# Attention with a learned position bias and a gated FFN on one Trainium2 core: where the split halves are made, how the PSUM places are cut, and bias rows computed by distance

## The chip, the cores and the metric

One core of a Trainium2 chip. The metric is the device time of one execution in microseconds (us); the kernel before has a median of 694.9 us over three runs.

## The reference, cut to what matters

Four batches, eight heads, 576 positions, 64 per head, all in fp32. The bias of a score depends on the query position i, on the distance |i - j| and on the head alone, so it is the same for all batches. The FFN has 2304 tokens, 512 in and out, 2048 hidden.

```python
scores = scale * np.matmul(q, k.transpose(0, 1, 3, 2))
psi_rel = np.log1p(np.abs(pos[:, None] - pos[None, :]))
psi_i = np.log1p(np.maximum(pos[:, None], 1.0))
x = (psi_rel / psi_i)[..., None]
h = np.maximum(x @ w1 + b1, 0.0)          # w1: 1 x 32
bias = h @ w2                             # w2: 32 x 8
scores = scores + bias.transpose(2, 0, 1)[None]
attn = softmax(scores)                    # sum + 1e-9
x = np.matmul(attn, v)                    # to 2304 x 512
h = x @ w_in
g = h * np.clip(h + 3.0, 0.0, 6.0) / 6.0
out = g @ w_out
```

## The kernel before, in words

**Engines.** PE is TensorE, DVE is VectorE, ACT is ScalarE, POOL is GpSimd, SP issues most loads. Where a product needs fp32 accuracy, both factors are split into a high and a low half (fp16, or the type `F32R` for q and k) and PE does three products: high x high, high x low, low x high. `high_part` (lines 117 to 123) makes a high half on POOL ("P"), DVE ("D") or ACT (any other letter); `low_part` (L140) makes a low half on DVE in one instruction, full x scale - high.

**Tiles.** The work is a list of softmax tiles n of 128 rows x 576 columns. First come rows 0 to 255 of the four batches, in units of one head pair with four tiles, then rows 256 to 575 of the four batches, in units with five tiles, the last of which holds 64 rows of each head. The rows 0 to 255 of batches 0 and 1 are "direct" tiles: `soft_max` (L559, DVE) adds the bias to the scores and takes the row maximum, `soft_exp` (L570, ACT) the exponential, PE turns the tile in fp32 through PSUM (`t_ps`), ACT copies it back. All 112 other tiles are normalised and split: `soft_norm` (L578, L582 on DVE, then the high half `hl`), `soft_low` (low half, L140), and `soft_turn` (L635) turns both by a DMA. Which engine makes `hl` follows the letters of `CFG['hl']`, tile by tile: 'AP' is ACT and POOL in turns.

**q and k** of a unit that is not direct come as one tile `st` of 832 (rows 0 to 255) or 896 columns. One tile ahead of the unit each, `split_qk_a` makes the high half `qkh` on ACT (L406), `split_qk_b` the low half `qkl` on POOL in two pieces, 576 columns of k and 256 or 320 of q (L413), and `split_qk_c` the two 64-column pieces `tq` of the last tile, on ACT (L426) and POOL (L427).

**The FFN** `ffn` (L736) of one batch and 256 or 320 tokens is a generator that is stepped from the main loop. The first layer has 16 hidden tiles of 12 matmuls `h_ps` (L781); for each, `post` issues ACT `t` (L771), DVE `t` (L764), ACT `g` (L758) and POOL `g` (L760). The second layer has 4 x 48 matmuls `o_ps` (L804). The first FFN is special: its second layer must wait until w_out is prepared, at whose end DVE forms `r_w2c`, the row ratios of w_out, with which the 16 tiles `g` are scaled again.

**Bias rows.** 36 groups of 16 query rows are computed once. `T` holds the table w1 x log1p|j - 572| over 1148 columns. `z_group` (L846 on DVE, L850 on ACT) makes four z tiles of 576 columns from shifted views of T, each with four query rows x 32 hidden units on its partitions; `bias_mm` (L863) multiplies them with w2, in fp32 (two passes, so 16 records a group), `bias_out` (L879) brings the result out of PSUM on ACT, `bias_store` writes it to tables `bias_d` in DRAM and `load_bias` loads 128 rows of a head pair on SP when a tile needs it. `bias_step` and `bias_next` do one step of this chain; the main loop calls them by the rates `rb` and others of `CFG`.

**PSUM** has 8 banks. `open_psum` begins with three double places (tag "s": scores, `t_ps`, bias) and two single places (tag "w": `h_ps`, `o_ps`, `pv_ps`). `open_banks` closes these and opens two double and four single places; from then on bias groups take two single places.

**Order.** The main loop runs `front(n)` and `back(n)` for each tile n, with FFN and bias steps between by credits. `START` = 21 opens the first FFN. At `SWITCH` = 37 `open_steady` runs what is left of the first FFN, opens the four single places and keeps PE's order as written from there; up to then a scheduler sorts each engine's instructions by priority.

```python
        if n == START:
            open_ffn()
        if n == cfg["psw"]:
            open_banks()
        if n == SWITCH:
            open_steady()
```

Of the kernel before, what the change touches and what calls it, by code (L numbers as in the profile page):

```python
# [1254 lines left out]
```

## Time and profile before

| | |
|---|---|
| runs | 693.82, 694.9, 696.72 us; median 694.9 |
| profiled execution, span | 690.7 us |
| PE busy | 640.2 us, 93% |
| DVE, ACT busy | 486.6 and 487.5 us, 70 and 71% |
| POOL busy | 261.1 us, 38% |
| largest groups on PE | `h_ps` 200.9 us, `o_ps` 195.5 us |
| bias groups on PE | `b_ps` 45.1 us of records, four column groups side by side |

The span is one execution as the hardware profiler took it on this core, from its first instruction to its last; the runs are timed without it. "PEld" is the loading of weights, which runs beside matmuls. An idle time is put down to what ended it. PEclk is the clock that TensorE was granted, as a share of its full one.

### The profile page before, as it was taken

The page shows a single profiled execution, that of the slowest core. Times are in us where ns is not written, and L with a number is a line of the kernel's source. Part 1 is how long each engine was busy: PE and PEld are TensorE (multiplying, and loading weights), DVE is VectorE, ACT ScalarE, POOL GpSimd, SP SyncE. Part 2 cuts the span into 40 slices and gives each one's busy share as a digit, 9 for nine tenths or more (in the row PEclk, how much of TensorE's full clock was granted, in tenths as well). Part 3 has the DMA queues.
Part 4 walks back from the last instruction along what each step waited for, and adds up shares of the span by engine and source line. Part 5 has one row for each costly group of instructions (what it writes and reads, how often), then busy time and mean ns, then how long its engine had stood idle before and what let it go on. Part 6 is the DMA issues. An engine that isn't in the chain of part 4 may idle for free. (4 is left out here: it accounts for less than half of the span.)

```text
span 690.7 us, 15099 instructions
## 1 busy us (share of the span) xinstructions
PE 640.2 (93%) x5552; PEld 453.1 (66%) x5552; DVE 486.6 (70%) x1150; ACT 487.5 (71%) x970; POOL 261.1 (38%) x322
## 2 busy tenths in 40 slices
PE   7688899787899999899989999999999999999998
PEld 2234456564587667578878877777767777777775
DVE  7889977999737977577778777876688668731310
ACT  7986768987739977697568857886688657832620
POOL 1111125756114532255335634653265425420420
PEclk9998999998999999999999999999999999999999
DMA  8899769651856798979999989787968795730000
GB/s 295 297 329 345 263 246 366 234 194 32 259 162 147 188 251 178 256 180 196 237 266 232 232 186 206 149 184 154 242 123 184 159 198 120 114 66 25 1 10 28
DMA packets 175737, 130.13 MB, mean 188 GB/s; under 512 B 137520, under 2 KB 144944, under 8 KB 174640
## 3 DMA queue, kind: packets, MB, share of 16 engines
q1 hardware_dynamic: 165872, 113.84, 66.0%
q10 hardware_dynamic: 9792, 15.34, 7.4%
q8 instruction: 43, 0.70, 0.4%
q14 instruction: 30, 0.25, 0.1%
HBM read 77.24 MB, written 15.34 MB: 134 GB/s over the span
## 5 line engine op out<-in xcount | busy, mean ns | idle before, releaser
L781 PE MATMUL h_ps<-x,wi 128*128 128x256 f16 (+1 forms) x1536 | 200.9, 288 | 8.7 <-DVE t L764 6.0
L804 PE MATMUL o_ps<-g,wo 128*128 128x256 f16 (+1 forms) x1536 | 195.5, 286 | 2.0 <-ACT g L123 1.3
L781 PEld LDWEIGHTS <-wi 128*128 128x128 f16 x1536 | 147.4, 98 | 60.9 <-issue 20.1
L804 PEld LDWEIGHTS <-wo 128*128 128x128 f16 x1536 | 147.3, 98 | 47.4 <-issue 10.5
L760 POOL TENSOR_TENSOR g<-t,g 128x256 f16<-128x256 f32 (+1 forms) x128 | 105.6, 834 | 154.9 <-ACT g L758 153.4
L570 ACT ACTIVATE bt<-bt,sm 128x576 f32<-128x576 f32 x144 | 110.6, 768 | 57.0 <-DVE sm L559 53.7
L140 DVE SCALAR_TENSOR_TENSOR hl<-bt,sm,hl 128x576 f16<-128x576 f32 x112 | 99.2, 900 | 30.1 <-ACT hl L123 14.7
L764 DVE SCALAR_TENSOR_TENSOR t<-t,t,h_ps 128x320 f32<-128x320 f32 (+1 forms) x112 | 56.0, 515 | 40.3 <-ACT t L771 39.2
L117 POOL TENSOR_SCALAR hl<-bt,sm 128x576 f16<-128x576 f32 x56 | 47.4, 847 | 94.9 <-DVE sm L582 30.1
L758 ACT ACTIVATE g<-t 128x256 f16<-128x256 f32 (+1 forms) x128 | 55.4, 438 | 31.8 <-DVE t L764 30.9
L559 DVE CUSTOM_DVE_ANT_0 bt<-s_ps,bt 128x576 f32<-128x576 f32 x88 | 64.5, 751 | 10.8 <-PE s_ps L527 5.4
L771 ACT ACTIVATE t<-h_ps,t,hr 128x320 f32<-128x320 f32 (+1 forms) x112 | 64.1, 586 | 6.1 <-PE h_ps L781 4.2
L413 POOL TENSOR_TENSOR qkl<-st,qkh 128x576 fp32r<-128x576 f32 (+2 forms) x48 | 57.9, 1229 | 24.3 <-ACT qkh L406 18.6
L863 PE MATMUL b_ps<-z_e,w_sb 128*32 128x288 f32 x448 | 45.1, 430 | 12.3 <-ACT bo L879 5.1
L814 ACT ACTIVATE ot<-o_ps,os 128x256 f32<-128x256 f32 (+1 forms) x32 | 15.9, 496 | 56.6 <-PE o_ps L804 51.4
L123 ACT ACTIVATE hl<-bt,sm 128x576 f16<-128x576 f32 x56 | 43.0, 770 | 7.2 <-DVE sm L582 4.2
L578 DVE TENSOR_SCALAR sm<-sm 128x1 f32<-128x1 f32 x112 | 16.7, 150 | 44.4 <-ACT bt L570 44.0
L846 DVE TENSOR_SCALAR z_e<-T,nbp 128x576 f32<-128x576 f32 x69 | 39.6, 622 | 11.6 <-PE b_ps L863 11.5
L879 ACT ACTIVATE bo<-b_ps,cv_sb,isc 128x288 f32<-128x288 f32 (+1 forms) x54 | 35.7, 663 | 2.9 <-DMA bias<-bo 2.0
L863 PEld LDWEIGHTS b_ps<-z_e,w_sb 128*32 128x32 f32 x448 | 14.8, 111 | 32.3 <-ACT z_e L850 6.6
L253 POOL TENSOR_SCALAR w<-w 128x1024 f32<-128x1024 f32 x8 | 10.8, 1348 | 65.3 <-ACT wo L252 52.9
L850 ACT ACTIVATE z_e<-T,bp 128x576 f32<-128x576 f32 x43 | 32.4, 771 | 3.9 <-DVE bp L1037 2.9
(125 smaller groups left out, 902.1 us busy)
## 6 DMA issues: line engine op xcount, KB each, us to landing
bt<-bias SPq DMA_DIRECT2D x36, 576.0 KB, 5.3
bias<-bo ACTq DMA_DIRECT2D x36, 288.0 KB, 5.6
w<-in_w_in_dram SPq DMA_DIRECT2D x8, 1024.0 KB, 7.2
vs<-in_vp_dram SPq DMA_DIRECT2D x24, 320.0 KB, 5.0
st<-in_qk_dram SPq DMA_DIRECT2D x16, 448.0 KB, 4.5
wo<-in_w_out_dram SPq DMA_DIRECT2D x5, 1024.0 KB, 5.1
bt<-bias SPq DMA_DIRECT2D x16, 288.0 KB, 3.6
qk<-in_qkd_dram SPq DMA_DIRECT2D x8, 544.0 KB, 8.9
```

The lines of the kernel that those rows point to most:

```text
L117: nc.gpsimd.tensor_scalar(out=out, in0=full, scalar1=scale, scalar2=1.0, op0=ALU.mult, op1=ALU.mult)
L140: nc.vector.scalar_tensor_tensor(out=out, in0=full, scalar=scale, in1=high, op0=ALU.mult, op1=ALU.subtract)
L413: nc.gpsimd.tensor_sub(out=lo[:, c:c + w], in0=t[:, c:c + w], in1=hi[:, c:c + w].bitcast(F32))
L559: nc.vector.tensor_tensor_reduce(out=halves(bt), in0=ps, in1=halves(src), op0=ALU.add, op1=ALU.min, scale=-0.125, scalar=3.0e38, accum_out ...
L570: nc.scalar.activation(out=bt, in_=bt, func=AF.Exp, scale=-1.0, bias=sm[:, 0:1], accum_out=total)
L758: nc.scalar.activation(out=g[:, 0], in_=uu, func=AF.Copy)
L760: e.tensor_sub(out=g[:, 1], in0=uu, in1=g[:, 0])
L764: nc.vector.scalar_tensor_tensor(out=t_t[f], in0=t_t[f], scalar=cols(f)[2], in1=h_t.pop(f)[:, 0:n], op0=ALU.min, op1=ALU.mult,)
L771: nc.scalar.activation(out=t_t[f], in_=h_t[f][:, 0:n], func=AF.Relu, scale=cols(f)[0], bias=cols(f)[1],)
L781: nc.tensor.matmul(out=h_t[f][:, 0:n], lhsT=wi[:, a, c, f * 128:(f + 1) * 128], rhs=x[:, e, c], start=(k == 0), stop=(k == 3 * KC - 1),)
L804: nc.tensor.matmul(out=ops[:, 0:n], lhsT=wo[:, a, f, e * 128:(e + 1) * 128], rhs=g_t[f][:, r], start=(f == 0 and a == 0 and r == 0), stop= ...
L863: nc.tensor.matmul(out=pss[a][32 * k:32 * k + 32, 0:HALF], lhsT=w2_sb, rhs=z[:, a * HALF:(a + 1) * HALF],)
```

## The change

Five things change.

1. `CFG['hl']` goes from 'AP' to 'A': the 56 high halves `hl` that POOL made are made by ACT.
2. `split_qk_b` makes `qkl` in one DVE instruction of the full width (832 or 896 columns); `split_qk_c` takes its low pieces to DVE and its high pieces from `qkh`.
3. `CFG['psw']` goes from 99 (never) to 21: `open_banks` runs at tile 21, beside `open_ffn`, not at tile 37.
4. Bias groups 16 to 35 (query rows from 256) are computed over distances, not columns. With `reach(g)` = the farthest distance to the left and to the right, the z tiles have max(reach) + 1 columns: 320, 304, 304, 320, 336 and so on to 576, and come from one table `dtab` = log1p(distance), which `distances` loads into `T` at tile 12 and multiplies by w1 on POOL. `bias_far` does one pass of four matmuls (two if there are more than 512 distances), ACT brings the result out forward for the right side and reversed for the left, and each row is stored as 591 columns that hold all 16 rows' windows; DRAM tables with skewed rows give each row its own window at the load. The load of a last tile becomes two DMAs.
5. `open_steady` puts a `bias_step` behind every second step of what is left of the first FFN.

```diff
@@ CFG
-'hl': 'AP'  'psw': 99
+'hl': 'A'  'psw': 21
@@ split_qk_b
-        for c, w in ((KC0[u], S), (QC0[u], QW[u])):
-            nc.gpsimd.tensor_sub(
-                out=lo[:, c:c + w], in0=t[:, c:c + w], in1=hi[:, c:c + w].bitcast(F32)
-            )
+        nc.vector.tensor_sub(out=lo, in0=t, in1=hi.bitcast(F32))
@@ split_qk_c
-            nc.scalar.activation(out=tz[rows, 0, rows], in_=t[rows, c], func=AF.Copy)
-            nc.gpsimd.tensor_sub(
+            nc.scalar.activation(
+                out=tz[rows, 0, rows], in_=hi[rows, c].bitcast(F32), func=AF.Copy
+            )
+            nc.vector.tensor_sub(
@@ load_bias
+        if 128 * i >= LATE:
+            m = 64 if i == 4 else 128
+            w = S + m - 1
+            table = table[:, m - 1:m - 1 + m * w].rearrange("h (i x) -> h i x", x=w)[:, :, 0:S]
         if i == 4:
-            d = dq("b").dma_start(out=out[:, 0:S], in_=table.rearrange("h i j -> (h i) j"))
+            for s in range(2):
+                d = dq("b").dma_start(out=out[64 * s:64 * s + 64, 0:S], in_=table[s])
@@ bias
+    def reach(g):
+        return 16 * g + 15, S - 1 - 16 * g
+
+    def distances():
+        nc.sync.dma_start(out=T[:, 0:S], in_=dtab)
+        nc.gpsimd.tensor_scalar(
+            out=T[:, 0:S], in0=T[:, 0:S], scalar1=w1_sb, scalar2=1.0, op0=ALU.mult, op1=ALU.mult
+        )
+
     def z_group(g):
+        n = S if g < EARLY else max(reach(g)) + 1
...
-            src = T[:, 572 - i0:572 - i0 + S]
+            src = T[:, 572 - i0:572 - i0 + S] if g < EARLY else T[:, 0:n]
...
+    def bias_far(g):
...
+        for a, lo in enumerate(range(0, n, 512)):
+            hi = min(lo + 512, n)
+            for k, z in enumerate(zs):
+                nc.tensor.matmul(
+                    out=pss[a][32 * k:32 * k + 32, 0:hi - lo], lhsT=w2_sb, rhs=z[:, lo:hi]
+                )
+            c = min(hi, front_ + 1)
+            if c > lo:
+                ev.append((slice(back + lo, back + c), pss[a][:, 0:c - lo]))
+            b, c = max(lo, 1), min(hi, back + 1)
+            ev.append((slice(back + 1 - c, back + 1 - b), pss[a][:, b - lo:c - lo][:, ::-1]))
+        bias_ps[g] = ev
@@ open_steady
-        while phase < 2:
+        for k in count():
+            if phase >= 2:
+                break
             ffn_step()
+            if k % 2 and emitted[3] < NG:
+                bias_step()
@@ main loop
+        if n == 12:
+            distances()
```

**The order on PE, up to the first `o_ps`.** Names: `b_ps` a bias group's place, `m_ps` a turned column of w_out's row maxima, `h_ps` and `o_ps` the FFN's two layers, `s_ps` scores, `t_ps` a turned direct tile, `pv_ps` attention times v. The kernel before:

```order
L863 MATMUL b_ps_1825<-z_e_114,w2_sb_103 32x288 x2
L153 MATMUL m_ps_1686<-eye_sb_93,m_w2_1684 128x128
L863 MATMUL b_ps_1825<-z_e_114,w2_sb_103 32x288 x6
L863 MATMUL b_ps_1901<-z_e_114,w2_sb_103 32x288
...
L781 MATMUL h_ps_1694<-x_745,wi_95 128x256
L863 MATMUL b_ps_1901<-z_e_114,w2_sb_103 32x288 x7
L804 LDWEIGHTS wo_96
L804 MATMUL o_ps_1769<-g_1156,wo_96 128x256
```

The changed kernel at the same place:

```order
L159 MATMUL m_ps_1695<-eye_sb_93,m_w2_1693 128x128
...
L791 MATMUL h_ps_1703<-x_745,wi_95 128x256
L628 MATMUL t_ps_1674<-eye_sb_93,bt_1217 128x128 x5
L557 MATMUL s_ps_1805<-qkh_1681 128x288 x2
L557 MATMUL s_ps_1805<-qkl_1730,qkh_1681 128x288 x2
L557 MATMUL s_ps_1805<-qkh_1681,qkl_1730 128x288 x2
L814 LDWEIGHTS wo_96
L814 MATMUL o_ps_1777<-g_1166,wo_96 128x256
...
L814 MATMUL o_ps_1777<-g_1185,wo_96 128x256
L887 MATMUL b_ps_1833<-z_e_114,w2_sb_103 32x320 x4
L670 MATMUL pv_ps_1889<-atf_1476,vf_1362 64x256
```

Two bias groups stood between the last `h_ps` of the first FFN and ahead of its first `o_ps`; now none does, and the first late group, of 320 columns, stands between `o_ps` matmuls. Counted over the list up to the first `o_ps`, 36 score matmuls on `qkh` and `qkl` became 30.

**The order on DVE, up to `r_w2c`.** The first `o_ps` needs it. `z_e` are z tiles, `w2p` and `wo` parts of w_out, `os` output scales. The kernel before:

```order
L846 TENSOR_SCALAR z_e<-T,nbp 128x576
...
L146 TENSOR_REDUCE m_w_1684<-w2p 128x1
L846 TENSOR_SCALAR z_e<-T,nbp 128x576 x2
L140 SCALAR_TENSOR_TENSOR hl<-bt,sm,hl 128x576 x2
L764 SCALAR_TENSOR_TENSOR t<-t,c_120,h_ps 128x256
L155 TENSOR_REDUCE p_w_1688<-m_ps 128x1
L140 SCALAR_TENSOR_TENSOR wo<-cu,w2s,wo 128x1024
...
L140 SCALAR_TENSOR_TENSOR hl<-bt,sm,hl 128x576
L214 RECIPROCAL rm_w_1690<-p_w_1688 128x1
...
L216 TENSOR_SCALAR r_w2c<-w2p,rm_w_1690 128x8
```

The changed kernel:

```order
L152 TENSOR_REDUCE m_w_1693<-w2p 128x1
L866 TENSOR_SCALAR z_e<-T,nbp 128x320
...
L146 SCALAR_TENSOR_TENSOR wo<-cu,w2s,wo 128x1024
L146 SCALAR_TENSOR_TENSOR hl<-bt,sm,hl 128x576
L161 TENSOR_REDUCE p_w_1697<-m_ps 128x1
...
L418 TENSOR_TENSOR qkl<-st,qkh 128x832
L220 RECIPROCAL rm_w_1699<-p_w_1697 128x1
...
L569 ISA bt,sm<-s_ps,k_529 128x576
...
L222 TENSOR_SCALAR r_w2c<-w2p,rm_w_1699 128x8
```

Counted over the list up to `r_w2c`, softmaxes went from 38 to 36, low parts of `hl` from 4 to 2, late z tiles from five of 576 columns to three of 320, and subtractions `qkl` from none to three.

**The order on ACT, in a five-tile unit beside an FFN's first layer.** `t` and `g` are the FFN's, `bt` the exponentials. The kernel before:

```order
L570 ACTIVATE bt,sm<-bt,sm 128x576 x2
L771 ACTIVATE t<-h_ps,t_1728,hr_2130 128x320
L123 ACTIVATE hl<-bt,sm 128x576
...
L758 ACTIVATE g<-t 128x320
...
L406 ACTIVATE qkh<-st 128x896
L426 ACTIVATE tq_104<-st 64x64 x2
```

The changed kernel:

```order
L580 ACTIVATE bt,sm<-bt,sm 128x576 x2
L781 ACTIVATE t<-h_ps,t_1736,hr_2153 128x320
L129 ACTIVATE hl<-bt,sm 128x576 x2
...
L768 ACTIVATE g<-t 128x320
...
L412 ACTIVATE qkh<-st 128x896
...
L429 ACTIVATE tq_104<-qkh 64x64 x2
```

Two high halves stand where one stood, ahead of the next `t` and `g`.

## Rows read from the trace of the kernel before

**Rows 1.** The page, part 1: busy us (share) xinstructions of each engine.

```profile
PE 640.2 (93%) x5552; PEld 453.1 (66%) x5552; DVE 486.6 (70%) x1150; ACT 487.5 (71%) x970; POOL 261.1 (38%) x322
```

**Rows 2.** Stages: length, then PE, PEld, DVE, ACT, POOL busy, PEclk, DMA.

```profile
100.00:177.34 77.34, 63.53 (x496) 42.23 (x493) 71.78 (x166) 63.64 (x121) 46.30 (x39) 0.96 0.61 202
177.34:204.06 26.72, 25.81 (x233) 21.05 (x232) 12.19 (x31) 12.59 (x23) 5.17 (x7) 1.00 0.77 223
204.06:310.00 105.94, 101.09 (x1064) 72.87 (x1064) 78.78 (x184) 87.90 (x180) 39.66 (x49) 0.98 0.84 194
310.00:610.00 300.00, 293.44 (x2633) 224.81 (x2632) 226.31 (x558) 221.28 (x481) 141.68 (x194) 0.99 0.88 186
610.00:690.70 80.70, 77.30 (x582) 55.34 (x579) 11.23 (x22) 22.02 (x44) 13.07 (x17) 1.00 0.07 21
```

**Rows 3.** DVE alone in 120:180 us, six windows of 10 us.

```profile
sum 60.00, DVE 58.62; mean DVE 9.77
```

**Rows 4.** Timeline of PE, 165:178 us: start, length, line, [idle <-releaser].

```profile
169.09 0.68 PE L863 MATMUL b_ps<-z_e,w_sb 128*32 128x288 f32 x4 [2.08 <-POOL vl L455]
177.34 1.47 PE L804 MATMUL o_ps<-g,wo 128*128 128x256 f16 x12 [1.13 <-ACT g L123]
```

**Rows 5.** Timeline of PE, bias groups (L863), 204:295 us.

```profile
204.06 1.18 PE L863 MATMUL b_ps<-z_e,w_sb 128*32 128x288 f32 x16
205.16 2.79 PE L781 MATMUL h_ps<-x,wi 128*128 128x256 f16 x24
292.22 0.68 PE L863 MATMUL b_ps<-z_e,w_sb 128*32 128x288 f32 x4 [2.68 <-ACT bo L879]
```

**Rows 6.** Timeline of ACT at 290 us.

```profile
290.73 0.52 ACT L426 ACTIVATE tq<-st 64x64 fp32r<-64x64 f32 x2 [4.33 <-DMA st<-in_qk_dram]
```

**Rows 7.** Groups of DVE by form: busy us, mean ns | idle before.

```profile
L559 DVE CUSTOM_DVE_ANT_0 bt<-s_ps,bt 128x576 f32<-128x576 f32 x88 | 64.5, 751 | 10.8 <-PE s_ps L527 5.4 <-DMA bt<-bias 3.2 <-PE s_ps L547 2.0
L140 DVE SCALAR_TENSOR_TENSOR hl<-bt,sm,hl 128x576 f16<-128x576 f32 x112 | 99.2, 900 | 30.1 <-ACT hl L123 14.7 <-POOL hl L117 14.5 <-DMA at<-hl 0.3
L140 DVE SCALAR_TENSOR_TENSOR vl<-vs,s_v,vh 128x640 f16<-128x640 f32 x24 | 24.6, 1025 | 3.2 <-ACT vh L123 3.2
L140 DVE SCALAR_TENSOR_TENSOR wi<-wo,w1s,wi 128x1024 f16<-128x1024 f32 x8 | 11.0, 1385 | 0.0
L846 DVE TENSOR_SCALAR z_a<-T,nbp 128x576 f32<-128x576 f32 x16 | 7.6, 520 | 0.1
```

**Rows 8.** Groups of ACT and of POOL by form: the high halves hl.

```profile
L123 ACT ACTIVATE hl<-bt,sm 128x576 f16<-128x576 f32 x56 | 43.0, 770 | 7.2 <-DVE sm L582 4.2 <-ACT g L758 1.3 <-ACT bt L570 1.1
L117 POOL TENSOR_SCALAR hl<-bt,sm 128x576 f16<-128x576 f32 x56 | 47.4, 847 | 94.9 <-DVE sm L582 30.1 <-ACT bt L570 19.7 <-DMA at<-hl 13.7
```

**Rows 9.** Timeline of DVE, four ops of 1024 columns.

```profile
124.43 2.48 DVE L140 SCALAR_TENSOR_TENSOR wo<-cu,w2s,wo 128x1024 f16<-128x1024 f32 x1
152.60 1.90 DVE L140 SCALAR_TENSOR_TENSOR wo<-cu,w2s,wo 128x1024 f16<-128x1024 f32 x1
163.22 1.69 DVE L263 SCALAR_TENSOR_TENSOR cu<-cu,z_e 128x1024 uint32<-128x1024 uint32 x1
172.69 1.27 DVE L140 SCALAR_TENSOR_TENSOR wo<-cu,w2s,wo 128x1024 f16<-128x1024 f32 x1
```

**Rows 10.** Timeline of POOL, low parts of q and k.

```profile
124.43 3.07 POOL L413 TENSOR_TENSOR qkl<-st,qkh 128x576 fp32r<-128x576 f32 x2 [0.66 <-ACT qkh L406]
284.11 2.10 POOL L413 TENSOR_TENSOR qkl<-st,qkh 128x576 fp32r<-128x576 f32 x2 [2.48 <-issue]
```

**Rows 11.** Two units, first layer of an FFN; columns as rows 2.

```profile
427.75:446.01 18.26, 18.26 (x157) 13.32 (x156) 14.86 (x37) 16.11 (x37) 12.21 (x16) 1.00 0.68 146
446.01:464.81 18.80, 18.12 (x155) 13.14 (x154) 15.15 (x36) 15.12 (x32) 10.51 (x16) 1.00 0.82 181
```

**Rows 12.** First unit of rows 11, hl tiles alone: DVE, ACT, POOL.

```profile
427.75:446.01 18.26, 4.28 (x5) 1.53 (x2) 2.23 (x3) 1.00 0.68 146
```

**Rows 13.** PE's waits, 200:691 us: total us, times, longest.

```profile
PE s_ps L547 <- DVE sm L559: 4.5, 4, 1.9
```

More of the change, by code (lines that the diff above doesn't have):

```diff
@@ L1 @@
 from contextlib import ExitStack, contextmanager, nullcontext
-from itertools import chain
+from itertools import chain, count
 import numpy as np
@@ L43, in attention_moe_kernel @@
     ltab: bass.AP,
+    dtab: bass.AP,
     psi: bass.AP,
@@ L104, in attention_moe_kernel @@
     wo = big.tile([128, 2, KF, DM], F16, name="wo")
-    bias_d = [dr_p.tile([H, min(128, S - i), S], F32, name=f"bias{i}") for i in range(0, S, 128)]
+    bias_d = [
+        dr_p.tile([H, 128, S] if i < LATE else [H, min(128, S - i) * (S + min(128, S - i))], F32, name=f"bias{i}")
+        for i in range(0, S, 128)
+    ]
     b1_sb = const.tile([128, 1], F32, name="b1_sb")
@@ L840, in z_group @@
             col = slice(i0 // 4, i0 // 4 + 1)
-            src = T[:, 572 - i0:572 - i0 + S]
+            src = T[:, 572 - i0:572 - i0 + S] if g < EARLY else T[:, 0:n]
             if k % 2 == 0:
                 z2 = (z_a if phase == 0 and g % 2 else z_e)[:, k // 2]
-            z = z2[:, (k % 2) * S:(k % 2 + 1) * S]
+            z = z2[:, (k % 2) * S:(k % 2) * S + n]
             if zeng(g, k) == "D":
@@ L852, in z_group @@
         bias_z[g] = zs
+    def bias_far(g):
+        zs = bias_z.pop(g)
+        back, front_ = reach(g)
+        n = max(back, front_) + 1
+        if four[0]:
+            pss = [w_bank("b_ps") for _ in range(0, n, 512)]
+        else:
+            ps = s_bank("b_ps")
+            pss = [ps[:, 0], ps[:, 1]]
+        ev = []
+        for a, lo in enumerate(range(0, n, 512)):
[10 more added lines that the diff above has]
+        bias_ps[g] = ev
     def bias_mm(g):
+        if g >= EARLY:
+            return bias_far(g)
         if four[0]:
@@ L870, in bias_out @@
         ps = bias_ps.pop(g)
-        t = hl_p.tile([128, S], F32, tag="hl", name="bo")
+        t = hl_p.tile([128, S + 16], F32, tag="hl", name="bo")
         c = pats.index(pattern(g))
         cv, sc = cv_sb[:, c:c + 1], isc[:, g:g + 1]
-        if isinstance(ps, list):
+        if g >= EARLY:
+            ev = [(t[:, c], src) for c, src in ps]
+        elif isinstance(ps, list):
             ev = [(t[:, a * HALF:(a + 1) * HALF], ps[a][:, 0:HALF]) for a in range(2)]
         else:
-            ev = [(halves(t), ps[:, :, 0:HALF])]
+            ev = [(halves(t[:, 0:S]), ps[:, :, 0:HALF])]
         for dst, src in ev:
             nc.scalar.activation(out=dst, in_=src, func=AF.Identity, scale=sc, bias=cv)
-        bias_t[g] = t
+        bias_t[g] = t[:, 0:S if g < EARLY else sum(reach(g)) + 1]
     def bias_store():
@@ L884, in bias_store @@
         r0 = (16 * g) % 128
-        dq("o").dma_start(
-            out=bias_d[g // 8][:, r0:r0 + 16].rearrange("h i j -> i h j"), in_=bias_t.pop(g)
-        )
+        t = bias_t.pop(g)
+        if g < EARLY:
+            table = bias_d[g // 8][:, r0:r0 + 16].rearrange("h i j -> i h j")
+        else:
+            m = 64 if g >= 32 else 128
+            c = m - 16 - r0
+            table = bias_d[g // 8].rearrange("h (i c) -> i h c", c=S + m)
+            table = table[r0:r0 + 16, :, c:c + t.shape[1]]
+        dq("o").dma_start(out=table, in_=t)
         emitted[3] += 1
@@ L1194, in attention_moe_kernel @@
     in_order.close()
-_INS = ["qk", "qkd", "vp", "w1c", "b1c", "w2b", "ltab", "psi", "ipsi", "eye", "w_in", "w_out"]
+_INS = ["qk", "qkd", "vp", "w1c", "b1c", "w2b", "ltab", "dtab", "psi", "ipsi", "eye", "w_in", "w_out"]
 def _layout(q, k, v, w1, b1, w2, moe_w_in, moe_w_out):
@@ L1222, in _layout @@
     pos = _np.arange(S).astype(_np.float32)
+    dtab = _np.broadcast_to(_np.log1p(pos), (128, S))
     psi = _np.log1p(_np.maximum(pos, _np.float32(1.0)))
@@ L1229, in _layout @@
         "qk": qk, "qkd": qkd, "vp": vp, "w1c": w1c, "b1c": b1c, "w2b": w2b,
-        "ltab": ltab.astype(_np.float32), "psi": psi, "ipsi": ipsi,
+        "ltab": ltab.astype(_np.float32), "dtab": dtab, "psi": psi, "ipsi": ipsi,
         "eye": _np.eye(128, dtype=_np.float32),
```

4 lines of the change are left out of this document (3 added, 1 removed).

## The prediction

> **What bounds the kernel now.** I read the page first, then a table by stage, then the time order of each engine where the table shows idle time. On the page TensorE (PE) is busy 640.2 of 690.7 us; VectorE (DVE), ScalarE (ACT) and GpSimd (POOL) stand at 486.6, 487.5 and 261.1 [rows 1]. That average hides different limits, so the rest goes by stage [rows 2]. The columns are time, then busy time of PE, PE's weight loads, DVE, ACT and POOL.
>
> From 100 to 177 us (tiles 21 to about 40: direct softmax tiles, the first layer of the first FFN, the preparation of w_out) PE is idle 77.3 - 63.5 = 13.8 us, and DVE works 71.8 of 77.3. Between 120 and 180 us DVE is busy 58.6 of 60 us [rows 3]. This stretch is bound by DVE, and it ends where `r_w2c`, the row ratio of w_out, lets the first `o_ps` matmul go, at 177.3 us [rows 4]. Just ahead of that PE waits 2.08 us and 1.13 us [rows 4].
>
> From 177 to 310 us PE idles 0.9 and then 4.9 us [rows 2]. More than half of the second part is one wait of 2.68 us before a bias group at 292.2 us [rows 5]. ACT was the late one there, because its queue stood 4.33 us behind a q/k load [rows 6]. From 310 to 610 us PE idles 300 - 293.4 = 6.6 us, and in the last 80.7 us it works alone [rows 2]. So from 177 us on, less PE work shortens the kernel one for one; before that, DVE must get less to do.
>
> **Part 1, bias rows by distance (20 of 36 groups).** A group takes 1.10 us on PE (204.06 to 205.16) for 576 columns [rows 5]. The new groups are 320, 304, 304, 320 and then up to 576 columns wide in steps of 16, together 8544 instead of 20 x 576 = 11520. In proportion this saves 20 x 1.10 x 0.258 = 5.7 us. The last four groups have a second, narrow piece with four weight loads more; between nothing and 0.45 us each, I take 0.13, 0.5 in all. Sum -5.2 us. On DVE and ACT the z tiles shrink by the same quarter, and an ACT eviction becomes two or three pieces of 591 columns in all; this is off PE's path while ACT has room (177 to 310 us: ACT 100.5 of 132.7 [rows 2]). The reversed PSUM read is in no row: it costs nothing, or at worst doubles its half of the evictions, 20 x 0.4 = 8 us at the rate of ACT's 576-column copy [rows 8], which would be hidden in the same 32 us of room. I take nothing. The early table is one load and one POOL pass of 576 columns, below 1 us as the POOL copies of that width [rows 8], on the least busy engine [rows 1]; SP waits for the last reader of T, and the loads behind it are for tiles six ahead. Nothing.
>
> **Part 2, POOL's low parts of q and k go to DVE.** On DVE an op with two SBUF inputs costs 1.03 us for 640 columns and 1.39 for 1024 [rows 7], so 832 and 896 columns lie near 1.2 and 1.27 us: 8 and 16 of them, 30 us over the whole span, and the 32 64-column pieces between 0 and 0.9 us each (0.9 is the 576-column op), taken at 0.3. Against that, DVE gets time back: beside a POOL subtraction that runs 3.07 us, the 1024-column DVE op took 2.48 us, at 152.6 us 1.90, and a third beside POOL's hl 1.69, where one alone takes 1.27 [rows 9, 10]. Those three alone are 1.2 + 0.6 + 0.4 = 2.3 us before `r_w2c`.
>
> In the stretch that DVE binds, what stands ahead of `r_w2c` changes, counted over DVE's list whose end is shown: three subtractions more (+3.6), two softmaxes less (2 x 0.75), two low parts hl less (2 x 0.90) [rows 7], and five z tiles of 576 become three of 320 (2.6 to 1.0 us, at 0.52 each [rows 7]): -1.3 us. With the 2.3 us the first `o_ps` comes 3.6 us earlier. But two bias groups and six score matmuls that filled PE's wait there now come behind it, where PE has no wait: 2 x 1.10 and, at 1.10 / 16 a pass, 0.4, so 2.6 us. Net -1.0 us.
>
> The trace shows both engines stretched: POOL's two subtractions take 3.07 us at 124 us and 2.10 at 284 [rows 10]. The Trainium skill, "SBUF — State Buffer", on who interferes with whom, says that a DVE instruction with two SBUF inputs and a GpSimd one that reads SBUF hold a shared port pair exclusively, so that the loser blocks for the whole instruction. By that rule the three removed POOL subtractions could give back up to their whole length instead of 2.3 us, which is rival (c); the DVE ops of [rows 9] show less than that.
>
> **Part 3, four single PSUM places from tile 21.** PE may run its h tiles ahead, so that ACT and DVE get the FFN's elementwise work earlier. DVE idles 5.5 us in this stretch [rows 2]: the gain lies between 0 and 5.5, and as DVE is full from 120 us on, I take 1.0. The price is that scores and transposes have two double places instead of three; it is bounded below by nothing, above by waits like the one of 2.08 us [rows 4], some two of them, 4.2 us. I take nothing and keep it as a rival.
>
> **Part 4, late bias rows spread.** Five groups move beside the 192 `o_ps` matmuls of 177 to 204 us, where DVE and ACT work 12.2 and 12.6 of 26.7 us [rows 2]. Later groups then have more lead. Of the 4.9 us of PE idle up to 310 us between 0 and all can go; the longest hangs on a load that no edit touches, so I take 2.0.
>
> **Part 5, all high halves by ACT.** 56 instructions of 0.85 us leave POOL and cost ACT 0.77 [rows 8], 43 us. What counts is the FFN's first layer: there a unit of five tiles lasts 18.3 and 18.8 us, ACT works 16.1 and 15.1, DVE 14.9 and 15.2 [rows 11], and POOL does up to three hl [rows 12]. With three and two more hl of 0.77 ACT comes to 18.4 and 16.7: over the first unit's length, inside the pair's. Nine such units take about 22 more copies. Between -4.5 us (PE's waits for DVE in this stretch disappear with the POOL collisions [rows 13]) and 22 x 0.77 = +16.9 us (none fits into ACT's waits), I take +1.5, since the second unit of each pair keeps 2 us free and the second layer's units have room to catch up.
>
> The split load of the last bias tile adds 16 issues on SP; its queue waits mostly for transposes, so nothing.
>
> **Sum.** -5.2 - 1.0 - 1.0 - 2.0 + 1.5 = -7.7 us against the span of 690.7: 683.0 us. The median of the runs, 694.9 us, is 4.2 above that span; with the same 4.2 the forecast is **687.2 us**, its own range 682 to 691.
>
> **Rivals.** (a) *ACT becomes the bound in the FFN's first layer.* Place: units like those two [rows 11]. It decides once the copies no longer fit into ACT's 2.2 to 3.7 us of idle time a unit, and much of that idle time is waits for DVE in ACT's own order. Full price: 687.2 - 1.5 + 16.9 = 702.6 us. Against it: PE ran without a wait in the first of these units although ACT was at 88%. The Trainium skill, "ScalarE: Activation LUTs", rules for kernel authors, speaks for it: multiplications belong on VectorE, not ScalarE. By that rule the copy is on the wrong engine; this trace has 0.77 us against 0.52 for a one-input DVE op of the same width. Chance 0.12.
>
> (b) *Two double places starve DVE.* The softmax of a direct tile waits for its scores and these for a place, and DVE's queue stands. Two waits of 2.1 us more, and the 1.0 of part 3 gone: 687.2 + 4.2 + 1.0 = 692.4 us (689 to 696). It is also the case in which the four places do not do what they say, since DVE, not PSUM, sets the first `o_ps`. Chance 0.15.
>
> (c) *The collisions were worth more.* Three POOL subtractions of 3.07 us [rows 10] last 9.2 us; were DVE held up all that time, 9.2 - 2.3 = 7 us more come off before `r_w2c`, and after 310 us -4.5 in place of +1.5: 687.2 - 7 - 6 = 674.2 us. For it: POOL's pieces are long and DVE was full. Chance 0.13.
>
> **Numbers.** The forecast has 0.60. A measurement of this kernel tells about 0.5% (3.5 us) from no change, so faster means below 691.4 and slower above 698.4. Faster: 0.60 + 0.13 + a quarter of (b) = 0.77. Same: the rest of (b) and a little of (a) = 0.13. Slower: 0.10. Leaving out the ends of (a) and (c), the range is 676 to 697 us.
>
> **What would show it.** Right: a bias group of 320 columns near 0.6 us on PE; the first `o_ps` near 174 us; DVE ops near 0.82 us instead of 0.90 for hl; PE idle from 310 us on below 9 us. Wrong: the first `o_ps` at 177 us or later with DVE idle before it, or PE waits behind ACT in the units of the FFN's first layer that add up to more than 10 us.

## The result, and the profile after

The changed kernel takes **684.26 us** (median of 4 runs, 683.93 to 685.09) against 695.08 (693.82 to 696.72): ratio 0.986, 95% interval 0.9839 to 0.9881. It is 1.4% faster, and in the range of 676 to 697. The forecast was 687.2. Its span of 682.2 us stands beside a forecast of 683.0; the rest of the miss is the 4.2 us added for the runs, since each execution of the experiments below outlasts its own span by 1.7 to 2.1 us only (683.93 against 682.2 for the changed kernel, whose profiled execution is one of its four runs). By that the execution behind the span of 690.7 lasted some 692.5 us (an estimate), less than any of the four runs before: a short one. So the change is worth 8.5 us by the two spans and 10.8 by the medians.

The page after, part 1, where [rows 1] stood:

```profile
PE 634.7 (93%) x5424; PEld 451.5 (66%) x5424; DVE 503.0 (74%) x1206; ACT 520.3 (76%) x1032; POOL 142.8 (21%) x187
```

The stages after, with the limits of [rows 2] (length, then PE, PEld, DVE, ACT, POOL busy, PEclk, DMA):

```profile
100.00:177.34 77.34, 68.10 (x474) 46.34 (x473) 71.15 (x168) 62.34 (x118) 30.87 (x31) 0.88 0.60 202
177.34:204.06 26.72, 26.72 (x236) 20.15 (x235) 11.57 (x28) 15.87 (x32) 1.65 (x3) 0.98 0.64 176
204.06:310.00 105.94, 101.71 (x1030) 75.62 (x1030) 82.88 (x209) 97.26 (x206) 20.89 (x33) 1.00 0.96 225
310.00:610.00 300.00, 292.98 (x2626) 224.23 (x2623) 240.24 (x592) 244.24 (x513) 60.74 (x86) 1.00 0.86 182
```

PE's work fell by 5.5 us and its idle time by 3.0. POOL lost 118 us, DVE and ACT gained 16 and 33. PE's timeline around the first `o_ps` (start, length, line, idle time before):

```profile
161.60 1.33 PE L628 MATMUL t_ps<-eye_sb,bt 128*128 128x128 f32 x5 [3.29 <-DVE sm L569]
172.43 0.74 PE L628 MATMUL t_ps<-eye_sb,bt 128*128 128x128 f32 x5 [1.50 <-DVE sm L569]
174.68 1.08 PE L814 MATMUL o_ps<-g,wo 128*128 128x256 f16 x6 [0.52 <-ACT g L129]
```

The first `o_ps` starts at 174.7 us; it was 177.3 [rows 4]. Stages by fixed times hide where the rest comes from, since the same work starts at other times. This table goes by places instead, all read from the starts of `h_ps` and `o_ps` on PE's timeline: A is the first `o_ps`, B the start of the third FFN's first layer, C that of the fifth. The span is that of the one execution that was profiled. The last column is the ratio by runs with its interval. The kernels below the first two are the experiments.

| kernel | A | A to B | B to C | C to end | span | ratio (95%) |
|---|---|---|---|---|---|---|
| before | 177.3 | 104.6 | 138.0 | 270.8 | 690.7 | 1 |
| changed | 174.7 | 107.7 | 127.3 | 272.5 | 682.2 | 0.986 (0.984 to 0.988) |
| u_columns | 173.4 | 112.0 | 127.5 | 272.7 | 685.6 | 0.994 (0.991 to 0.996) |
| u_hl | 175.6 | 103.8 | 128.4 | 272.4 | 680.2 | 0.982 (0.979 to 0.985) |
| u_qk | 171.2 | 109.1 | 126.4 | 271.3 | 678.0 | 0.982 (0.979 to 0.985) |
| u_psw | 177.0 | 108.1 | 127.3 | 272.6 | 685.0 | 0.9945 (0.993 to 0.996) |
| u_spread | 174.0 | 105.1 | 136.1 | 272.5 | 687.7 | 0.994 (0.992 to 0.997) |
| u_hl_qk | 173.7 | 108.0 | 128.8 | 270.9 | 681.4 | 0.9825 (0.980 to 0.985) |
| b_psw | 174.4 | 110.5 | 137.7 | 270.7 | 693.3 | 0.998 (0.996 to 1.001) |
| n_early8 | 173.6 | 107.5 | 128.3 | 271.2 | 680.6 | 0.986 (0.983 to 0.988) |
| u_psw_spread | 178.3 | 104.3 | 134.5 | 272.5 | 689.6 | 0.997 (0.995 to 0.9995) |
| b_dist | 179.1 | 103.9 | 133.2 | 270.8 | 687.0 | 0.9875 (0.984 to 0.991) |
| n_mix1 | 173.0 | 105.1 | 128.6 | 272.7 | 679.4 | 0.982 (0.979 to 0.985) |
| n_mix2 | 174.3 | 105.1 | 128.3 | 270.8 | 678.5 | 0.979 (0.976 to 0.982) |

So between before and changed: 2.7 us gained up to A, 3.1 lost from A to B, where 19 late bias groups now stand instead of 14, 10.7 gained from B to C, and 1.7 lost from C to the end. The 10.7 us are three things. Before, B to C held 6.35 us of `b_ps`, now 2.15: 4.2 us. PE's idle time falls from 7.9 to 3.9: 4.1 us. And PE's other work takes 2.4 us less (123.7 and 121.3 us), while the granted clock rises from 0.98 to 1.00 of 138 us, which is some 2.8 us by the same rows. B to C in the kernel before, all work and then `b_ps` on PE alone:

```profile
281.90:419.90 138.00, 130.08 (x1280) 105.64 (x1279) 101.77 (x250) 100.17 (x222) 63.86 (x88) 0.98 1.00 221
```

```profile
281.90:419.90 138.00, 6.35 (x64) 0.98 1.00 221
```

The changed kernel in the same piece of the program:

```profile
282.40:409.70 127.30, 123.45 (x1236) 103.14 (x1232) 103.98 (x265) 108.41 (x236) 24.67 (x40) 1.00 1.01 230
```

```profile
282.40:409.70 127.30, 2.15 (x21) 1.00 1.01 230
```

### The profile page after: what moved, and what is told of

Its sections match the earlier page's. It is cut to its first block, busy times and chain, and to the rows that moved or that the text cites. A ratio compares the mean times of both kernels' runs of the same rounds, so it can differ in the third digit from the quotient of the medians.

```text
span 682.2 us, 14758 instructions
## 1 busy us (share of the span) xinstructions
PE 634.7 (93%) x5424; PEld 451.5 (66%) x5424; DVE 503.0 (74%) x1206; ACT 520.3 (76%) x1032; POOL 142.8 (21%) x187
## 5 line engine op out<-in xcount | busy, mean ns | idle before, releaser
L146 DVE SCALAR_TENSOR_TENSOR hl<-bt,sm,hl 128x576 f16<-128x576 f32 x112 | 90.7, 827 | 25.6 <-ACT hl L129 24.4
L129 ACT ACTIVATE hl<-bt,sm 128x576 f16<-128x576 f32 x112 | 83.8, 769 | 8.2 <-DVE sm L592 2.8
L146 DVE SCALAR_TENSOR_TENSOR x<-pv_ps,xr,x 64x320 f16<-64x320 f32 (+3 forms) x56 | 23.6, 445 | 20.0 <-ACT x L730 19.0
L866 DVE TENSOR_SCALAR z_e<-T,nbp 128x576 f32<-128x576 f32 (+17 forms) x69 | 31.5, 502 | 8.5 <-PE b_ps L887 8.5
L926 ACT ACTIVATE bo<-b_ps,cv_sb,isc 128x576 f32<-128x576 f32 (+36 forms) x60 | 36.0, 640 | 1.8 <-PE b_ps L887 1.8
L628 PE MATMUL t_ps<-eye_sb,bt 128*128 128x128 f32 x160 | 26.9, 304 | 10.4 <-DVE sm L569 6.4
L460 POOL MEMSET vl<- 64x128 f16 x24 | 5.0, 209 | 148.2 <-DVE vl L146 107.8
L628 PEld LDWEIGHTS t_ps<-eye_sb,bt 128*128 128x128 f32 x160 | 19.3, 153 | 20.7 <-ACT atf L631 6.7
L716 PE MATMUL pv_ps<-at,vh 128*64 128x320 f16 (+1 forms) x432 | 32.0, 293 | 0.7 <-DVE t L774 0.7
L870 ACT ACTIVATE z_e<-T,bp 128x576 f32<-128x576 f32 (+17 forms) x43 | 29.2, 698 | 4.1 <-DVE bp L1090 3.3
```

The lines of the kernel that those rows point to most:

```text
L129: nc.scalar.activation(out=out, in_=full, func=AF.Copy, scale=scale)
L146: nc.vector.scalar_tensor_tensor(out=out, in0=full, scalar=scale, in1=high, op0=ALU.mult, op1=ALU.subtract)
L628: nc.tensor.transpose(tp[:, 128 * c:128 * c + 128], bt[:, j:j + 128], eye_sb)
L716: nc.tensor.matmul(out=ps[64 * s:64 * s + 64, 0:n], lhsT=w[:, 128 * c + 64 * s:128 * c + 64 * s + 64], rhs=at[:, c, s * n:(s + 1) * n], st ...
```

## The experiments

Of their names, "u_" is the changed kernel with a part undone, "b_" the kernel before with a part alone, "n_" a new mixture. A ratio's interval is some 2 us wide to each side. A row of the table is one execution, and not always a typical one: those of u_psw, u_columns, n_early8 and u_qk are the shortest of their runs and those of b_dist, u_hl and u_hl_qk the longest, 1.0 to 2.9 us from their medians. So a step of 2 us is believed here where a place of the table shows it in several kernels. From C to the end it is so: 270.7 to 271.3 us in seven of the kernels, 272.4 to 272.7 in the other seven.

### The bias rows by distance

u_columns undoes them:

```diff
-EARLY = 16
+EARLY = 36
...
-        if n == 12:
-            distances()
```

> The changed kernel with all 36 bias groups by columns (576 wide, unskewed tables, no early table, no reversed eviction); everything else as changed. My theory (a group's PE time is proportional to its columns, 1.10 us for 576, and PE is the bound where the late groups stand): 5.2 us slower than the changed kernel's 684.3, about 689.5 us, ratio to the kernel before near 0.992. Rival (the b_ps records fill 30.2 us of PE before and 20.3 us after, so the rows by distance are worth about 10 us): 694 us, ratio 0.999. Second rival (the gain on PE is eaten by ACT's extra evictions): 684 to 686 us.

It came to 689.2 us, ratio 0.9938, that is 5.4 us above the changed kernel at the 693.4 us of before on that chip (the split load of a last tile stays). b_dist adds them alone (with the split load of a last tile and the copy from `qkh`):

> The kernel before with the bias rows by distance alone (early table, reversed evictions, skewed tables, split last load); PSUM places, spread and engines as before. My theory (PE's columns alone, one for one): 5.2 us faster than before, ratio 0.9925. Rival (the late groups then stand where ACT and DVE bind, or PE still waits at 290 us): 0.997 to 1.000.

It came to 685.9 us, ratio 0.9875: 8.7 us by runs (6.3 to 11.0), 3.7 us by spans. The profiled execution is the longest of its six (688.8, the median 685.9), so its span says too little: the median spans of all runs, 684.1 against 691.6, differ by 7.5 us. In the profile the first `o_ps` comes 1.8 us later than before, and from there to the end it is 507.9 us against 513.4, so 5.5 us shorter. That fits the theory; where its typical execution gains more is not shown. The groups themselves, on PE's timeline of the changed kernel:

```profile
187.03 0.72 PE L887 MATMUL b_ps<-z_e,w_sb 128*32 128x304 f32 x8
199.02 0.75 PE L887 MATMUL b_ps<-z_e,w_sb 128*32 128x320 f32 x8
205.04 0.77 PE L887 MATMUL b_ps<-z_e,w_sb 128*32 128x336 f32 x8
253.77 1.01 PE L887 MATMUL b_ps<-z_e,w_sb 128*32 128x480 f32 x8
```

A group of 576 columns takes 1.18 us by the same kind of row [rows 5]. From 0.72 for 304 to 1.01 for 480 it is 0.0016 us a column; along that line the twenty groups sum to 18.5 us against 23.6: 5.1 us saved. The reversed half of an eviction costs what a forward one does, on ACT by form:

```profile
L926 ACT ACTIVATE bo<-b_ps,cv_sb,isc 128x319 f32<-128x319 f32 x1 | 0.6, 607 | 0.0
L926 ACT ACTIVATE bo<-b_ps,cv_sb,isc 128x320 f32<-128x320 f32 x1 | 0.6, 603 | 0.0
L926 ACT ACTIVATE bo<-b_ps,cv_sb,isc 128x303 f32<-128x303 f32 x1 | 0.6, 595 | 0.0
L926 ACT ACTIVATE bo<-b_ps,cv_sb,isc 128x304 f32<-128x304 f32 x1 | 0.6, 587 | 0.0
```

(319 and 303 columns are reversed, 320 and 304 forward; one instruction each.)

### High halves by ACT

u_hl undoes them:

```diff
-'hl': 'A'
+'hl': 'AP'
```

> The changed kernel with the high halves of every second tile back on POOL. My theory (ACT's 56 more copies cost 1.5 us net of the collisions they remove): 682.8 us. Rival (collisions of POOL with DVE's two-input ops were worth more than predicted): 4.5 us or more slower, 689 us or above, with DVE's low parts hl back from 0.83 to 0.87 us or more. Third: no change within 2 us, since ACT has the room.

680.8 us, ratio 0.982: 2.8 us faster than the changed kernel (0.004 of 693.4). The size is near the forecast term, the place is not: from C to the end nothing changes (272.4 against 272.5), and A to B becomes 3.9 us shorter, of which A (0.9 later) and B to C (1.1 longer) take 2.0 back. The stretch 206 to 246 us, where the second FFN's first layer meets bias groups, in the kernel before, the changed one and u_hl, in this order:

```profile
206.00:246.00 40.00, 38.90 (x420) 28.42 (x419) 34.52 (x81) 36.71 (x78) 17.67 (x23) 1.00 0.73 168
```

```profile
206.00:246.00 40.00, 36.35 (x366) 26.45 (x364) 33.70 (x87) 39.05 (x84) 11.03 (x16) 1.00 0.82 196
```

```profile
206.00:246.00 40.00, 38.86 (x393) 28.58 (x392) 35.34 (x94) 39.38 (x86) 14.70 (x22) 1.00 0.90 208
```

ACT is nearly full in all three, 36.7 to 39.4 of 40 us. In the changed kernel PE gets 36.35 us of work done beside it, with POOL's turns back 38.86. Eight high halves stand on ACT there, four in u_hl. PE's waits read "DVE t" (in total, times, longest us), but DVE works only 33.7 of 40 and waits itself for ACT's high halves. The changed kernel, then u_hl:

```profile
PE h_ps L791 <- DVE t L774: 2.6, 4, 1.1
DVE hl L146 <- ACT hl L129: 3.8, 4, 1.4
```

```profile
PE h_ps L791 <- DVE t L774: 0.2, 1, 0.2
DVE hl L146 <- ACT hl L129: 1.9, 2, 1.6
```

Other kernels bear it out. From its first `h_ps` to its first `o_ps` the second FFN takes 39.4 us in the changed kernel and 40.1 in u_qk, where ACT makes all high halves, and 36.5 to 38.3 in u_hl, u_hl_qk, n_early8, n_mix1 and n_mix2, where POOL makes half. It is not the copies alone: u_spread, with all of them on ACT but no late groups brought forward, takes 37.5. B to C goes the other way: 126.4 to 127.5 us in the changed kernel, u_columns, u_qk and u_psw, 128.3 to 128.8 in the five with POOL's turns.

### The low parts of q and k

u_qk puts them back on POOL (with the 64-column low pieces, not shown):

```diff
-        nc.vector.tensor_sub(out=lo, in0=t, in1=hi.bitcast(F32))
+        for c, w in ((KC0[u], S), (QC0[u], QW[u])):
+            nc.gpsimd.tensor_sub(
+                out=lo[:, c:c + w], in0=t[:, c:c + w], in1=hi[:, c:c + w].bitcast(F32)
+            )
```

> The changed kernel with the low parts of q and k back on POOL in two pieces (the 64-column high pieces still from qkh). My theory: 1 us slower, 685.3 us, first o_ps within 2 us of 174.7. Rival (c) of the prediction (DVE blocked for the whole of POOL's subtractions): 7 us slower, 691 us, first o_ps near 180. Other side: DVE is freed of 16 us, so faster, 681 us.

680.7 us, ratio 0.982: 2.8 us faster, where 1 us slower was expected. The first `o_ps` comes at 171.2, 3.5 us earlier than with the subtractions on DVE, and C to the end is 1.2 us shorter. DVE from 100 to 177 us by form, the changed kernel:

```profile
L146 DVE SCALAR_TENSOR_TENSOR wo<-cu,w2s,wo 128x1024 f16<-128x1024 f32 x6 | 8.7, 1458 | 1.1 <-ACT wo L129 0.7 <-DMA wo<-in_w_out_dram 0.3
L272 DVE SCALAR_TENSOR_TENSOR cu<-wo,cu 128x1024 uint32<-128x1024 uint32 x5 | 6.6, 1314 | 0.0
L269 DVE SCALAR_TENSOR_TENSOR cu<-cu,wo 128x1024 uint32<-128x1024 uint32 x4 | 4.9, 1216 | 1.6 <-POOL wo L139 1.6
L269 DVE SCALAR_TENSOR_TENSOR cu<-cu,z_e 128x1024 uint32<-128x1024 uint32 x3 | 3.6, 1216 | 0.0
L272 DVE SCALAR_TENSOR_TENSOR cu<-z_e,cu 128x1024 uint32<-128x1024 uint32 x3 | 4.0, 1332 | 0.0
L418 DVE TENSOR_TENSOR qkl<-st,qkh 128x832 fp32r<-128x832 f32 x3 | 3.5, 1169 | 0.0
```

u_qk, the same, and its pieces on POOL:

```profile
L146 DVE SCALAR_TENSOR_TENSOR wo<-cu,w2s,wo 128x1024 f16<-128x1024 f32 x6 | 8.4, 1403 | 0.5 <-ACT wo L129 0.2 <-DMA wo<-in_w_out_dram 0.2
L272 DVE SCALAR_TENSOR_TENSOR cu<-wo,cu 128x1024 uint32<-128x1024 uint32 x5 | 7.0, 1401 | 0.0
L269 DVE SCALAR_TENSOR_TENSOR cu<-cu,wo 128x1024 uint32<-128x1024 uint32 x4 | 6.0, 1500 | 1.6 <-POOL wo L139 1.6
L269 DVE SCALAR_TENSOR_TENSOR cu<-cu,z_e 128x1024 uint32<-128x1024 uint32 x3 | 4.4, 1467 | 0.0
L272 DVE SCALAR_TENSOR_TENSOR cu<-z_e,cu 128x1024 uint32<-128x1024 uint32 x3 | 4.0, 1328 | 0.0
L419 POOL TENSOR_TENSOR qkl<-st,qkh 128x576 fp32r<-128x576 f32 x3 | 5.7, 1892 | 13.0 <-ACT qkh L412 13.0
L419 POOL TENSOR_TENSOR qkl<-st,qkh 128x256 fp32r<-128x256 f32 x2 | 2.4, 1222 | 0.0
```

The 21 two-input DVE ops of 1024 columns take 27.8 us without POOL's subtractions and 29.8 with them: the move gave DVE 2.0 us back and cost it 3.5. That is 1.5 of the 3.5 us. The rest is order: in u_qk DVE's list up to `r_w2c` holds 34 softmaxes instead of 36, 1.5 us at 0.75 each [rows 7], and only two units' subtractions run ahead of the first `o_ps`. The third comes behind it:

```profile
176.81 1.41 POOL L419 TENSOR_TENSOR qkl<-st,qkh 128x576 fp32r<-128x576 f32 x1 [12.46 <-ACT qkh L412]
```

Ahead of the first `o_ps`, then, POOL's pieces ran 6.6 us, and these DVE ops lost 2.0. The Trainium skill, "SBUF — State Buffer", on who interferes with whom, has the loser blocked for the whole instruction; here the stretch as a whole shows three tenths of that. The softmaxes beside POOL's pieces took 0.75 us, as they do elsewhere [rows 7].

u_hl_qk undoes both moves off POOL:

> The changed kernel with both moves off POOL undone: every second high half and the low parts of q and k back on POOL; what is left of the change is bias by distance, PSUM places from tile 21 and the spread. Each undone alone made it 2.8 us faster, in different stretches (the halves between 206 and 246 us, the subtractions before the first o_ps). If these gains are independent (ACT's room and DVE's room): 5.6 us faster than the changed kernel, ratio 0.978. Rival (POOL's collisions with DVE return once both are on POOL, hl back to 0.90 us): no better than either alone, 0.982, or back to 0.986.

681.3 us, ratio 0.9825: no better than either alone, though 2.4 us better than the changed kernel. So the two costs of 2.8 us do not add: each was measured with the other move in place. The low parts `hl` on DVE show the collisions. Their mean goes 900 ns before [rows 7], 827 changed, 855 in u_qk, 869 in u_hl and 888 here; the changed kernel's row and this one's:

```profile
L146 DVE SCALAR_TENSOR_TENSOR hl<-bt,sm,hl 128x576 f16<-128x576 f32 x112 | 90.7, 827 | 25.6 <-ACT hl L129 24.4
```

```profile
L146 DVE SCALAR_TENSOR_TENSOR hl<-bt,sm,hl 128x576 f16<-128x576 f32 x112 | 98.2, 888 | 27.1 <-ACT hl L129 13.3 <-POOL hl L123 12.3 <-DMA out_dram<-ot 0.9
```

Those 7.5 us of DVE's time cost the kernel less than the two moves did, since u_hl_qk is the faster one.

### PSUM places and the spread

u_psw opens the four single places at tile 37 again; b_psw opens them at 21 in the kernel before; u_spread takes the bias steps out of `open_steady`; u_psw_spread does both removals.

```diff
-'psw': 21
+'psw': 99
```

```diff
-            if k % 2 and emitted[3] < NG:
-                bias_step()
```

> The changed kernel with the four single PSUM places opened at tile 37 as before. My theory: 1.0 us slower, 685.3 us. Rival (two double places starve DVE: PE waits for DVE's softmax ahead of t_ps for 6.4 us before 177 us in the changed kernel, 1.4 before): 3 to 5 us faster, 680 us, with those waits gone and the granted clock between 100 and 177 us back from 0.88 to 0.96.

> The kernel before with the four single PSUM places at tile 21 alone. By the prediction's step: 1.0 us faster than before, ratio 0.9985. By what its removal cost (5.8 us by the medians, 2.8 by the spans): ratio 0.992 to 0.996, with the first o_ps about 2 us earlier. Rival: alone it does nothing or harm, since two late bias groups stand ahead of the first o_ps and each now takes two of the four single places: ratio 1.000 to 1.005.

> The changed kernel without the bias step behind every second step of what is left of the first FFN. My theory: the late groups fall behind again and PE waits for one of them or for a bias load before 310 us: 2.0 us slower than the changed kernel, ratio to the kernel before near 0.989. Rival: the spread does nothing, since the groups by distance are cheap enough to be caught up: within 1 us, ratio 0.986.

> The changed kernel with neither the PSUM places at tile 21 nor the spread. Each of the two left out alone cost about 5.8 us by the medians. If they are two independent gains: 11.6 us slower than the changed kernel, ratio to the kernel before near 1.003. If they are one gain that needs both (a bias step between o_ps matmuls needs single places to go to, and single places alone only start the first o_ps earlier): about 6 us slower, 0.994 to 0.995.

u_psw: 689.5 us, ratio 0.9945, 5.9 us slower by runs and 2.8 by spans; its profiled execution is the shortest of twelve (686.8), and that one loses at A (177.0 against 174.7) and little beyond. b_psw: ratio 0.998, 1.1 us faster, which fits the forecast step of 1.0 us but is not told from nothing (0.996 to 1.001); its first `o_ps` is 2.9 us earlier, and A to B is 5.9 us longer. What the places do is seen in DVE's order up to `r_w2c`: softmaxes, low parts `hl` and late z tiles are 38, 4 and 5 before and 38, 4 and 6 in u_psw, but 35, 2 and 3 in b_psw. In the changed kernel they are 36, 2 and 3, with the subtractions on DVE. So the shorter DVE list that the prediction put down to the moves off POOL comes with the PSUM places; the move of the subtractions adds a softmax or two to it. The first `o_ps` of u_psw and of b_psw:

```profile
176.98 0.83 PE L814 MATMUL o_ps<-g,wo 128*128 128x256 f16 x6
```

```profile
174.38 0.85 PE L804 MATMUL o_ps<-g,wo 128*128 128x256 f16 x3
```

u_spread: 689.5 us, ratio 0.994, 5.8 us slower where 2.0 was expected. A to B is 2.6 us shorter, B to C 8.8 longer: the groups that do not stand beside the first `o_ps` stand at 279 to 320 us. There ACT works 38.6 of 41 us, PE waits 5 us, and behind the wait that ends at 303.58 the granted clock falls. The window, and the two longest waits on PE's timeline:

```profile
279.00:320.00 41.00, 35.92 (x366) 27.45 (x365) 31.48 (x77) 38.59 (x85) 11.14 (x18) 0.96 0.92 224
```

```profile
284.78 2.78 PE L791 MATMUL h_ps<-x,wi 128*128 128x256 f16 x24 [1.88 <-DVE t L774]
303.58 7.07 PE L791 MATMUL h_ps<-x,wi 128*128 128x256 f16 x48 [2.04 <-DVE t L774]
```

u_psw_spread: 691.4 us, ratio 0.997, 7.7 us slower. By runs the two are neither one gain (5.8 expected) nor two of 5.8 (11.6), but something between. By spans 2.8 and 5.5 make 8.3, near the 7.4 measured, but with u_psw's shortest execution in the sum that shows little. The places differ: leaving out the one costs at A, the other between A and C.

### Mixtures

n_early8 is u_hl_qk with `EARLY = 8`, the distance table loaded at the start, and the other table cut to the part that groups 0 to 7 need:

```diff
-EARLY = 16
+EARLY = 8
-            src = T[:, 572 - i0:572 - i0 + S] if g < EARLY else T[:, 0:n]
+            src = T[:, S + 124 - i0:S + 124 - i0 + S] if g < EARLY else T[:, 0:n]
```

> The kernel u_hl_qk with groups 8 to 15 by distance as well (448 to 336 columns instead of 576, their eviction in two pieces, the distance table loaded at the start in place of the part of the other table that no group needs). If the bias groups of the first 50 us are bound by PE, DVE and ACT together as they stand (DVE and ACT busy 83% there): PE has 8 x 1.10 x 0.32 = 2.8 us less, DVE 2.6 us less, so 1 to 2.5 us faster than u_hl_qk. Rival: the longer chain to the first groups and 16 evictions instead of 8 on ACT eat it: the same or 1 us slower.

683.7 us, ratio 0.986: 2.3 us slower than u_hl_qk by runs, which is worse than the rival had it. PE works 76.8 us of the first 100 instead of 79.0, and the first `o_ps` comes at 173.6 instead of 173.7: PE's columns do not set that stage. What does, and where the 2.3 us go, is not shown.

n_mix1 is u_hl with `qkl` of the first three units that need it on POOL; n_mix2 has those of the five-tile units there too, and the 64-column low pieces:

```diff
-        nc.vector.tensor_sub(out=lo, in0=t, in1=hi.bitcast(F32))
+        if u or b == 2 and p < 3:
+            for c, w in ((KC0[u], S), (QC0[u], QW[u])):
+                nc.gpsimd.tensor_sub(
+                    out=lo[:, c:c + w], in0=t[:, c:c + w], in1=hi[:, c:c + w].bitcast(F32)
+                )
+        else:
+            nc.vector.tensor_sub(out=lo, in0=t, in1=hi.bitcast(F32))
```

> The changed kernel with every second high half back on POOL, and the first three low parts of q and k (those ahead of the first o_ps) back on POOL; the other low parts stay on DVE. If the first stretch is bound by DVE's 3 x 1.02 us of subtractions and 204 to 310 us by ACT: the first o_ps near 171.5 as with the subtractions on POOL, then 232 us to the fifth FFN as with the halves on POOL, then 272.4: a span near 676, some 4 us below either alone, ratio 0.976 to 0.978. Rival (the order that the scheduler makes of the first 180 us decides, and not the engine): 0.981 to 0.985.

> As n_mix1, with the low parts of q and k of the five-tile units on POOL too, so that DVE keeps only the other five units of the first kind. If DVE and ACT bind a little in the five-tile units: 1.5 us below n_mix1 (270.9 in place of 272.4 us from the fifth FFN on). Rival: collisions take it back: the same as n_mix1.

n_mix1: 681.5 us, ratio 0.982, no better than u_hl: its first `o_ps` came at 173.0, not 171.5. That fits the rival: with the first subtractions on POOL, A is 171.2, 173.0, 173.7 and 174.3 in four kernels here, so the order made by priorities counts as much as the engine. n_mix2: **679.3 us, ratio 0.979 (0.976 to 0.982)**, 2.2 us below n_mix1 where 1.5 was expected, and from C to the end, where the difference was forecast, 1.9 us shorter (270.8 against 272.7). It is the fastest kernel here, faster than both given ones:

```profile
PE 638.9 (94%) x5424; PEld 454.5 (67%) x5424; DVE 484.2 (71%) x1155; ACT 486.0 (72%) x976; POOL 246.4 (36%) x313
```

POOL at 36% and DVE and ACT at 71 and 72% is a better share of the work here than 21, 74 and 76%.

## Why the prediction was right, point by point

- **Part 1 (-5.2 us): right.** PE's rows give 5.1 us, the removal 5.4, b_dist 5.5 from the first `o_ps` on (by runs alone, 6.3 or more). The mark was off: a group of 304 to 320 columns takes about 0.72 to 0.75 us, not 0.6; the rows lie on a line that does not go through zero, 0.0016 us a column and 0.24 fixed.
- **Part 2 (-1.0): the step that failed.** Its own terms were sized well: three subtractions +3.5 us (forecast +3.6), collisions -2.0 (forecast -2.3). But the step also claimed the fewer softmaxes, low parts and z tiles ahead of `r_w2c`, 4.9 us, which the order showed for the whole change and which belong to the PSUM places. Without them the move costs: 2.8 us by the runs of u_qk; by its places 3.5 at the first `o_ps`, 1.2 from C on, and 0.5 back in between (4.2 by its span). With the high halves back on POOL it is 1.3 to 2.6 us at the first `o_ps` (u_hl against n_mix2, u_hl_qk and n_mix1), and it costs nothing that the runs can tell (u_hl 0.982, u_hl_qk 0.9825); the cost from C on stands in all seven kernels that have the subtractions of the five-tile units on DVE.
- **Part 3 (-1.0): fits alone, too small in company.** b_psw measured 1.1 us, with an interval that holds zero. In the changed kernel the places are worth 5.9 us by runs and 2.8 by the spans. b_psw loses what it gains at A again before B; the changed kernel keeps it. That the other parts make the room for it is likely, not shown.
- **Part 4 (-2.0): too small.** 5.8 us by runs, 5.5 by spans. The step counted PE's idle time alone; the groups that come late also stand between B and C as work of PE (4.78 us of `b_ps` in u_spread, 2.15 in the changed kernel), fill ACT there, and in u_spread's execution the clock fell as well.
- **Part 5 (+1.5): right in sign, near in size (2.8), wrong in place.** It was costed in the five-tile units, where u_hl shows nothing from C on; the 1.7 us lost from C on go with `qkl` on DVE (u_qk and n_mix2 win most or all of them back). The cost lies at 206 to 246 us, ahead of those units, where the step did not look. The prediction had read ACT's room from 177 to 310 us as 100.5 of 132.7 us busy (in part 1), a mean [rows 2] that hid 40 us at 92% (36.71 of 40).
- **The sum** was -7.7; -8.5 by spans and -10.8 by medians was measured. Part 2 was 3.8 us too good and parts 3 and 4 together 5 us or so too bad (-7.7 by the removal of both), so the total is right partly by luck: errors of opposite sign met. The runs themselves add up: 5.4 for part 1, 7.7 for parts 3 and 4, less the 2.4 that both moves cost together, make 10.7.
- **The marks.** The first `o_ps` came at 174.7 us (174 forecast), for another reason than the one given, and `hl` at 827 ns (0.82). PE's idle time from 310 us on was to fall below 9 us; it is 10.6, and 10.0 before.
- **The rivals.** (a), ACT as the bound, is the mechanism of part 5's cost, but over a stretch of 40 us and not over nine units. (b), fewer double places: the waits are there (3.29 and 1.50 us for DVE's softmax ahead of `t_ps`), but DVE is busy all through both, and the first `o_ps` comes earlier, not later. (c), collisions: they took 7.5 us of `hl` time alone, but only 2.0 before `r_w2c`; it falls with u_qk, which was faster where (c) had it 7 us slower.

What stays open: where the typical executions of b_dist and u_psw differ from the profiled ones. By runs they gain 8.7 and lose 5.9 us, by spans 3.7 and 2.8; the profiled ones are the longest of six and the shortest of twelve. Open too is why the costs of the two moves off POOL do not add.

## What to carry to other kernels

A diff of several parts has one order. To say which part moved an instruction, build each part alone and count its order again: here that alone would have put most of the shorter DVE list under the PSUM places. Cover is to be read in the stretch in which the new work lands, not over the stage: an engine at 76% over 133 us was at 92% for 40. And moving work to a faster instruction on a fuller engine was a loss here where that engine's list was what PE waited for; the best kernel here gave POOL work back. One profiled execution is one draw: its span should be held against the runs before a difference of 2 or 3 us is read from it.
